# Five of the 32 float64 pieces narrowed among the retention's tiles in written order, the other 27 spread wider

## The chip, the cores and the metric

The kernel runs on one core of a Trainium2 chip. The metric is the device time of one execution in microseconds (us); lower is better. The core has TensorE (PE, matrix products), VectorE (DVE), ScalarE (ACT), GpSimd (POOL) and SyncE (SP), which issues most transfers. Each engine works through its own queue in order; they wait for each other by semaphores.

## What is computed

Three stages follow one another. A retention (attention with a decay instead of a softmax) over 4 x 8 heads of 576 positions gives 2304 tokens of 512 features. A mixture of 8 experts gives each token to one expert, at most 288 to each, by the order of all logits. A dense layer with a gate ends it; its weights w_in and w_out come as float64 words, the others as float32.

```python
rel = pos[:, None] - pos[None, :]
Dmat = np.where(rel >= 0, gamma[:, None, None] ** rel[None, :, :], 0.0)
x = np.matmul(scale * np.matmul(q, k.transpose(0, 1, 3, 2)) * Dmat, v)   # per head, then 2304 x 512
...
for idx in np.argsort(-(x @ w_gate).flatten()):                          # greedy, 288 tokens per expert
    ...
for e in range(E):
    out[mask] = np.maximum(x[mask] @ w1[e], 0.0) @ w2[e]
...
h = out @ w_in                                                           # w_in, w_out: float64
g = h * np.tanh(np.log1p(np.exp(h)))
return (g @ w_out).astype(np.float32)
```

## The kernel before

**Retention (0 to 82 us).** 18 tiles of 128 tokens, two in each pass of the loop `for o in range(2, NT, 2)`. For a tile t: `load` brings qk and kv (512 KB each, on SyncE), `scores` multiplies queries and keys on TensorE and puts the mask on with VectorE (am, L200), `scale` makes qs and ks on GpSimd (L185, L188), `carried` and `outputs` form the output pT from the running state S and from am, ScalarE copies it (xT, L238), `state` adds to S (L214, VectorE), `turn` turns xT into rows of tokens with the router's logits (pX, L248; L, L250 on VectorE; xs, L252 on ScalarE), `store` sends xs to DRAM. TensorE, VectorE, GpSimd and SyncE take this stage's instructions in the order in which the code is written (`manual_schedule`).

**Routing (82 to 119 us).** The greedy order is found by a serial chain of short steps, mostly on VectorE (L394 to L541), with tiny products on TensorE (small). It starts in the last pass of the retention for the first 16 tiles (L380 to L406, G) and goes on after the last logits. After the first expert is known, the steps for the next ones (known, sat, scan, ohb, pI, chosen) run beside the experts.

**Experts (119 to 362 us).** For each expert GpSimd gathers its 288 tokens (xg, L651), TensorE turns them (mmx, L672), ScalarE and VectorE split them into a high and a low part (xh L662, xl L664), and TensorE multiplies in three passes: 96 products mma for the first layer (then hh on ScalarE, hl on VectorE), 96 products mmb for the second, whose result y is copied by ScalarE (L849) out of one of five banks. Weights come in units of 512 KB (st, issued by SyncE at L588); ScalarE makes whi (L602) of each, VectorE or GpSimd wlo (L605), which frees the place of st. The last units (`final_units`) are the narrowed w_in and w_out.

**Narrowing.** w_in and w_out are 32 pieces of 128 x 512 float64 numbers (512 KB). One piece takes a load std (L762, issued on ScalarE's queue for the piece three further on), words on ScalarE (L779, a copy of the high words with a scale), a shift on VectorE (L781), a join with the low words on VectorE (dw, L784), the sign on ScalarE (dt, L788), a product with the sign on GpSimd (L798), and a store of 256 KB into a scratch tensor in DRAM (L767). All 32 are done beside the experts.

The order from the routing on is made by a planner when the program is built (`run_tasks`): of the tasks that can start, it takes the one that starts first by its own table of durations, unless one of higher priority comes soon. Narrowing has the low priority 4 and rises to `UP` when the number of narrowed pieces falls behind TensorE's planned time (`PACE` per piece, `START`). Transfers issued by SyncE and ScalarE take turns on eight completion semaphores, so an issue can wait for the landing of the transfer eight places before it, whichever of the two queues that was on.

```python
    def narrow_priority(self):
        return UP if len(self.features) >= URGENT or len(self.narrowed) * PACE + START < self.time.get(PE, 0) else 4
```

Of the kernel before, what the change touches and what calls it, by code (L numbers as in the profile page):

```python
# [7 lines left out]
F32 = mybir.dt.float32  # L8
# [3 lines left out]
U32 = mybir.dt.uint32  # L12
# [42 lines left out]
EID = -2  # L55
PACE = 8000
START = 50000
# [76 lines left out]
class Kernel:  # L134
# [3 lines left out]
    def attention(self):  # L138
# [7 lines left out]
        with ExitStack() as st:  # L146
# [3 lines left out]
            ps = st.enter_context(tc.tile_pool(name="ps", bufs=1, space=PSUM))  # L150
            st.enter_context(tc.manual_schedule(engines={mybir.EngineType.PE, mybir.EngineType.DVE, mybir.EngineType.Pool, mybir.EngineType.SP}))
            dec = one.tile([P, DCN], F32, name="dec")
# [103 lines left out]
            def store(t):  # L256

                if t in XS:
                    nc.sync.dma_start(a["x"][t * P:(t + 1) * P, :], XS.pop(t))
# [36 lines left out]
            for o in range(2, NT, 2):  # L296
                b = o + 1
                load(o + 4)
                load(o + 5, "qk")
                if o + 4 >= NT:  # L300
                    for t in range(o):
                        store(t)
                scores(b)
                carried(o)
                carried(b)
                scores(b + 1)
                if o == 6:
# [12 lines left out]
                if b < NT - 1:  # L320
                    state(b)
                outputs(b)
                if b + 1 < NT - 1:
                    state(b + 1)
                turn(o)
                if b < NT - 1:
                    turn(b)
            t = b
            self.psum = lambda name, shape: ps.tile(shape, F32, name=name, tag="pS", bufs=1)
# [3 lines left out]
            for i in range(NT):  # L333
                store(i)
            self.choices(late, choice)
            self.reached(choice, G, late)
# [342 lines left out]
    def narrow_priority(self):  # L679
        return UP if len(self.features) >= URGENT or len(self.narrowed) * PACE + START < self.time.get(PE, 0) else 4  # L680

# [55 lines left out]
    def step(self, t, done):  # L737
        try:
            t[0] = t[1].send(done)
        except StopIteration:  # L740
            self.tasks.remove(t)

    def narrow(self):

        nc, v, ic, a = self.nc, self.nc.vector, self.ic, self.a
        done = {k: {} for k in ("load", "read", "turn", "shift", "sign", "store")}

        def at(k, n):
            return [lambda: done[k].get(n)] if n >= 0 else []

        name = ("w_in", "w_out")
        words, sent = {}, {}

        def place(n):
            c, r = divmod(n // 2, a[name[n % 2]].shape[0] // P)
            return name[n % 2], slice(r * P, r * P + P), c

        def fetch(n, queue):
            if n < 32:
                w, r, c = place(n)  # L760
                words[n] = self.conv.tile([P, 512, 2], U32, name="std", bufs=3)
                queue.dma_start(words[n].rearrange("p c w -> p (c w)"), a[w].bitcast(U32)[r, c * 1024:c * 1024 + 1024])  # L762

        def send(n, queue):
            if n >= 0:
                w, r, c = place(n)
                queue.dma_start(a[w + "32"][r, c * 512:c * 512 + 512], sent.pop(n))  # L767

        def load():
            now = yield SP, 3 * DMA_ISSUE, [Event(0)], self.narrow_priority  # L770
            for n in range(3):
                fetch(n, nc.sync)
                self.spawn(piece(n, self.arrival(524288, now, LATE)))

        def piece(n, now):
# [15 lines left out]
            fetch(n + 3, nc.scalar)  # L791
            if n:
                self.narrowed[n - 1] = done["store"][n - 1] = self.arrival(262144, sign, LATE)
# [367 lines left out]
```

## Time and profile before

| what | value |
|---|---|
| median of 3 runs | 790.85 us (790.5 to 792.45) |
| profiled execution | 792.95 us, span of its instructions 791.2 us |
| TensorE busy | 749.2 us, 95% |
| VectorE busy | 672.9 us, 85% |
| ScalarE busy | 405.5 us, 51% |
| GpSimd busy | 488.1 us, 62% |
| moved by DMA | 111.94 MB, 141 GB/s over the span |

The span runs from the first to the last instruction of the profiled execution; its time is that of the whole execution. A row of a timeline gives the start in us from the span's start, the duration in us, engine, line and operation, and in square brackets the idle time of the engine ahead of the instruction and what ended it.

### The profile page before, as it was taken

What the parts mean: (1) busy time and instruction counts of PE and PEld (TensorE: products, weight loads), DVE (VectorE), ACT (ScalarE), POOL (GpSimd) and SP (SyncE); (2) the same over time, 40 slices, a digit from 0 to 9 for tenths busy, and PEclk for the clock granted to TensorE, in tenths of its full rate; (3) what the DMA queues carried; (4) which work ended last, traced back from release to release, by engine and by line L of the source; (5) the groups of instructions that cost most, each with busy time, mean ns of one, the idle gap of its engine ahead of it and who ended that gap; (6) DMA issues with size and microseconds to landing.
All of it is one profiled execution on the core that took longest, in us unless ns stands there. A gap on an engine that the chain in (4) does not pass through costs nothing.

```text
span 791.2 us, 15556 instructions
## 1 busy us (share of the span) xinstructions
PE 749.2 (95%) x5892; PEld 679.0 (86%) x5892; DVE 672.9 (85%) x1079; ACT 405.5 (51%) x783; POOL 488.1 (62%) x408
## 2 busy tenths in 40 slices
PE   7999379999999999799999999999999999999995
PEld 5999239899898999799998999899999989998983
DVE  4445788888898888777999999989999998998993
ACT  2333025646556475757764465546555554655451
POOL 6651036979788797430577586557557655756554
PEclk9999699999999999999999999999999999999998
DMA  9887085888888888986500011010001001001001
GB/s 359 327 291 268 28 271 185 278 266 281 274 291 278 273 279 270 334 283 213 174 22 22 1 50 31 1 41 30 12 1 51 31 0 41 21 1 40 1 1 40
DMA packets 60539, 111.94 MB, mean 141 GB/s; under 512 B 4784, under 2 KB 32432, under 8 KB 60464
## 3 DMA queue, kind: packets, MB, share of 16 engines
q1 hardware_dynamic: 44240, 73.45, 27.4%
q10 hardware_dynamic: 13248, 28.06, 10.1%
q0 software_dynamic: 2976, 9.44, 3.7%
q8 instruction: 46, 0.75, 0.4%
q14 instruction: 29, 0.24, 0.1%
HBM read 88.38 MB, written 22.54 MB: 140 GB/s over the span
## 4 chain that ended last, share of the span: by engine, by line
PE 46%; DVE 12%; DMA 2%; ACT 2%; issue 1%; POOL 1%; ACTq 0%; POOLq 0%; SPq 0%; DVEq 0%
PE mmc L1038 20%; PE po L1099 19%; DVE q L1068 6%; PE mma L815 4%; DVE n L1063 3%; PE mmb L815 2%; DMA st<-w 1%; ACT whi L602 1%; DVE n L1073 1%; DVE wlo L605 1%; DMA q<-y_scratch 1%; POOL gl L1080 1%; POOL n L1070 0%; DVE G L472 0%; DVE words L781 0%
## 5 line engine op out<-in xcount | busy, mean ns | idle before, releaser
L1068 DVE RECIPROCAL q<-q 128x384 f32<-128x384 f32 x96 | 243.8, 2540 | 0.1
L1070 POOL TENSOR_TENSOR n<-n,q 128x384 f32<-128x384 f32 x96 | 101.1, 1054 | 161.6 <-DVE q L1068 142.7
L605 POOL TENSOR_TENSOR wlo<-st,whi 128x1024 fp32r<-128x1024 f32 x51 | 122.4, 2414 | 16.7 <-ACT whi L602 11.7
L1038 PE MATMUL mmc<-yh,whi 128*128 128x384 f32 x384 | 129.6, 337 | 1.0 <-DVE n L1073 1.0
L1038 PE MATMUL mmc<-yl,whi 128*128 128x384 f32 x384 | 129.9, 338 | 0.2 <-DVE yl L998 0.2
L1038 PE MATMUL mmc<-yh,wlo 128*128 128x384 f32 x384 | 129.4, 337 | 0.0
L1078 ACT CAST gh<-n 128x384 fp32r<-128x384 f32 x96 | 49.3, 513 | 148.3 <-DVE n L1073 141.0
L1080 POOL TENSOR_TENSOR gl<-n,gh 128x384 fp32r<-128x384 f32 x96 | 120.2, 1254 | 3.6 <-ACT gh L1078 3.5
L1063 DVE SCALAR_TENSOR_TENSOR n<-s 128x384 f32<-128x384 f32 x96 | 114.9, 1198 | 5.2 <-POOL gl L1080 3.9
L1099 PE MATMUL po<-whi,gl 128*128 128x512 f32 x288 | 114.9, 399 | 1.4 <-POOL gl L1080 1.0
L1099 PE MATMUL po<-whi,gh 128*128 128x512 f32 x288 | 114.5, 397 | 0.7 <-ACT gh L1078 0.7
L1099 PE MATMUL po<-wlo,gh 128*128 128x512 f32 x288 | 113.9, 396 | 0.0
L602 ACT CAST whi<-st 128x1024 fp32r<-128x1024 f32 x80 | 82.7, 1044 | 34.7 <-issue 23.7
L815 PE MATMUL mma<-xh,whi 128*128 128x288 f32 x256 | 77.9, 304 | 3.4 <-ACT xh L662 2.6
L815 PE MATMUL mma<-xl,whi 128*128 128x288 f32 x256 | 77.3, 302 | 1.9 <-DVE xl L664 1.9
L815 PE MATMUL mmb<-hl,whi 128*128 128x288 f32 x256 | 77.3, 302 | 0.0
L815 PE MATMUL mmb<-hh,whi 128*128 128x288 f32 x256 | 77.1, 301 | 0.0
L815 PE MATMUL mma<-xh,wlo 128*128 128x288 f32 x256 | 77.1, 301 | 0.0
L1038 PEld LDWEIGHTS mmc<-yh,whi 128*128 128x128 f32 x384 | 72.1, 188 | 5.3 <-DVE n L1073 1.4
L1038 PEld LDWEIGHTS mmc<-yl,whi 128*128 128x128 f32 x384 | 72.1, 188 | 4.5 <-DVE yl L998 0.4
L815 PE MATMUL mmb<-hh,wlo 128*128 128x288 f32 x256 | 75.9, 296 | 0.0
L1038 PEld LDWEIGHTS mmc<-yh,wlo 128*128 128x128 f32 x384 | 72.1, 188 | 0.0
(153 smaller groups left out, 1548.9 us busy)
## 6 DMA issues: line engine op xcount, KB each, us to landing
st<-w SPq DMA_DIRECT2D x64, 512.0 KB
qk<-qk SPq DMA_DIRECT2D x18, 512.0 KB
kv<-kv SPq DMA_DIRECT2D x18, 512.0 KB
std<-w_out ACTq DMA_DIRECT2D x15, 512.0 KB
std<-w_in ACTq DMA_DIRECT2D x14, 512.0 KB
x_scratch<-xs SPq DMA_DIRECT2D x18, 256.0 KB
y_scratch<-y ACTq DMA_DIRECT2D x32, 144.0 KB
yt<-y_scratch SPq DMA_DIRECT2D x22, 192.0 KB
```

What stands on the lines that cost most here:

```text
L602: self.nc.scalar.copy(dst[0], st)
L605: (self.nc.vector if lo.engine == DVE else self.nc.gpsimd).tensor_tensor(dst[1], st, dst[0].bitcast(F32), op=ALU.subtract)
L815: self.nc.tensor.matmul(bank[1][:, :CAP], al if h == 2 else ah, bl if h == 1 else bh, start=(first and j == h == 0), stop=(last and j == n ...
L1038: self.nc.tensor.matmul(bank[1][:, :TILE], (wl if h == 2 else wh)[:, c, cs], x[c][h == 1], start=(c == h == 0), stop=(c == HP - 1 and h == 2))
L1063: v.scalar_tensor_tensor(u, s, 2.0, s, op0=ALU.subtract, op1=ALU.mult)
L1068: v.reciprocal(q, q)
L1070: nc.gpsimd.tensor_tensor(u, u, q, op=ALU.mult)
L1073: v.tensor_tensor(u, u, p, op=ALU.mult)
L1078: nc.scalar.copy(gh, u)
L1080: nc.gpsimd.tensor_tensor(gl, u, gh.bitcast(F32), op=ALU.subtract)
L1099: nc.tensor.matmul(po[j], (gl if h == 2 else gh)[:, js], (wl if h == 1 else wh)[:, f % 2], start=(f == h == 0), stop=(f == DFF // P - 1 an ...
```

## The change

`EARLY` = 5 pieces (n = 0 to 4) are narrowed in the retention, one for each pass from o = 8 to o = 16 (`FROM` = 8). `early_pieces` returns five steps, which the loop calls at fixed places: `load_piece(o + 2)` and `send_piece(o - 2)` on SyncE behind the next tiles' loads, `shift(o)` on VectorE between the mask products of the pass's two tiles, `join(o)` on VectorE between its two copies of S, with the product by the sign on GpSimd behind it, and `widths(o + 2)` (words and sign) on ScalarE at the end of the pass. The last store stands behind the stores of x. ScalarE's order in the retention is now the written one too. The early pieces have tiles of their own (est 3, ewords 2, edt 1, edw 3). The planner does the other 27, with `PACE` at 9500 instead of 8000, counted from `EARLY` on.

```diff
-PACE = 8000
+PACE = 9500
+EARLY = 5
+FROM = 8
...
                 load(o + 4)
                 load(o + 5, "qk")
+                load_piece(o + 2)
+                send_piece(o - 2)
...
                 carried(o)
                 carried(b)
+                shift(o)
                 scores(b + 1)
...
                 if b < NT - 1:
                     state(b)
+                join(o)
                 outputs(b)
...
                 turn(o)
                 if b < NT - 1:
                     turn(b)
+                    widths(o + 2)
...
             for i in range(NT):
                 store(i)
+            send_piece(b - 1)
...
-        return UP if len(self.features) >= URGENT or len(self.narrowed) * PACE + START < self.time.get(PE, 0) else 4
+        return UP if len(self.features) >= URGENT or (len(self.narrowed) - EARLY) * PACE + START < self.time.get(PE, 0) else 4
...
+        def load(n):
+            st[n] = pool.tile([P, 512, 2], U32, name="est", bufs=3)
+            nc.sync.dma_start(st[n].rearrange("p c w -> p (c w)"), self.piece_of(n)[0])
+
+        def widths(n):
+            high = st[n][:, :, 1].bitcast(F32)
+            words[n] = pool.tile([P, 512], F32, name="ewords", bufs=2)
+            nc.scalar.activation(words[n], high, AF.Copy, scale=2.0 ** -112)
+            sign[n] = pool.tile([P, 512], F32, name="edt", bufs=1)
+            nc.scalar.sign(sign[n], high)
+
+        def shift(n):
+            w = words[n].bitcast(U32)
+            nc.vector.tensor_scalar(w, w, self.ic[:, IC["three"]], None, op0=ALU.logical_shift_left)
+
+        def join(n):
+            o = pool.tile([P, 512], U32, name="edw", bufs=3)
+            nc.vector.scalar_tensor_tensor(o, st[n][:, :, 0], self.ic[:, IC["low"]], words[n].bitcast(U32),
+                                           op0=ALU.logical_shift_right, op1=ALU.bitwise_or)
+            out[n] = o.bitcast(F32)
+            nc.gpsimd.tensor_tensor(out[n], out[n], sign[n], op=ALU.mult)
...
+        def step(of):
+            def run(o):
+                if 0 <= (o - FROM) // 2 < EARLY:
+                    of((o - FROM) // 2)
+            return run
...
-            for n in range(3):
+            for n in range(EARLY, EARLY + 3):
                 fetch(n, nc.sync)
```

In the orders that follow, those after carry the line numbers of the changed code. VectorE in the pass o = 14 of the retention, before (am the mask products, S the state, L the logits):

```order
L200 TENSOR_TENSOR am<-pA_88,mask_81 128x512
L200 TENSOR_TENSOR am<-pA_89,mask_81 128x512
L200 TENSOR_TENSOR am<-sc,mask_81 128x512
L200 TENSOR_TENSOR am<-pA_88,mask_81 128x512
L214 TENSOR_TENSOR S<-pS,dec 128x256 x2
L250 TENSOR_REDUCE L<-pX 128x8 x2
```

And after (ewords is what the shift works on, edw the join's result):

```order
L203 TENSOR_TENSOR am<-pA_91,mask_84 128x512
L203 TENSOR_TENSOR am<-pA_92,mask_84 128x512
L776 TENSOR_SCALAR ewords<-ewords,consts 128x512
L203 TENSOR_TENSOR am<-sc,mask_84 128x512
L203 TENSOR_TENSOR am<-pA_91,mask_84 128x512
L217 TENSOR_TENSOR S<-pS,dec 128x256
L780 SCALAR_TENSOR_TENSOR edw<-est,consts,ewords 128x512
L217 TENSOR_TENSOR S<-pS,dec 128x256
L253 TENSOR_REDUCE L<-pX 128x8 x2
```

The shift has come ahead of the third mask product, the join between the two copies of S.

VectorE in the last pass, before, from its last mask products over the routing's first steps (G is the last of them) to the last logits:

```order
L200 TENSOR_TENSOR am<-pA_89,mask_81 128x512
L200 TENSOR_TENSOR am<-sc,mask_81 128x512
L380 TENSOR_SCALAR sc<-consts 128x194
L394 TENSOR_REDUCE sc<-L 128x16
L396 TENSOR_TENSOR sc<-L,sc 128x128
L397 TENSOR_TENSOR sc<-sc,consts 128x128
L398 TENSOR_REDUCE top<-sc 128x16
L399 TENSOR_TENSOR oh<-sc,top 128x128
L406 TENSOR_TENSOR G_123<-sc,consts 128x16x63
L250 TENSOR_REDUCE L<-pX 128x8 x2
L394 TENSOR_REDUCE sc<-L 128x2
```

And after:

```order
L203 TENSOR_TENSOR am<-pA_92,mask_84 128x512
L203 TENSOR_TENSOR am<-sc,mask_84 128x512
L776 TENSOR_SCALAR ewords<-ewords,consts 128x512
L389 TENSOR_SCALAR sc<-consts 128x194
L403 TENSOR_REDUCE sc<-L 128x16
L405 TENSOR_TENSOR sc<-L,sc 128x128
L406 TENSOR_TENSOR sc<-sc,consts 128x128
L407 TENSOR_REDUCE top<-sc 128x16
L408 TENSOR_TENSOR oh<-sc,top 128x128
L415 TENSOR_TENSOR G_126<-sc,consts 128x16x63
L780 SCALAR_TENSOR_TENSOR edw<-est,consts,ewords 128x512
L253 TENSOR_REDUCE L<-pX 128x8 x2
```

The shift has come ahead of the routing's first step, the join between G and the last two rows of logits.

ScalarE where expert 5 ends and expert 6 begins, before (y the last copy of expert 5's result, xh the tokens of expert 6, dt, words and the DMA of w_in, w_out and std the narrowing, whi a weight unit, hh the first result of expert 6):

```order
L849 COPY y<-mmb_5221 128x288
L851 DMA y_scratch<-y 128x288
L662 CAST xh<-mmx_5328 128x288
L662 CAST xh<-mmx_5336 128x288
L662 CAST xh<-mmx_5341 128x288
L662 CAST xh<-mmx_5346 128x288
L788 ACTIVATE dt<-std 128x512
L767 DMA w_in<-dw 128x512
L762 DMA std<-w_in 128x1024
L602 CAST whi<-st 128x1024
L838 ACTIVATE hh<-mma_5356 128x288
```

And after:

```order
L671 CAST xh<-mmx_5335 128x288
L671 CAST xh<-mmx_5340 128x288
L671 CAST xh<-mmx_5345 128x288
L671 CAST xh<-mmx_5350 128x288
L836 ACTIVATE dt<-std 128x512
L815 DMA w_out<-dw 128x512
L811 DMA std<-w_out 128x1024
L827 ACTIVATE words<-std 128x512
L897 COPY y<-mmb_5258 128x288
L899 DMA y_scratch<-y 128x288
```

The last y copy has moved from ahead of xh to behind a piece's fetch (DMA std) and words.

TensorE at the same place, before (mmb the last product of expert 5, mmx the turning of tokens, mma expert 6's first layer):

```order
L815 MATMUL mmb_5221<-hh,wlo 128x288
L672 MATMUL mmx_5328<-consts,xg 128x96 x3
L672 MATMUL mmx_5336<-consts,xg 128x96 x3
L672 MATMUL mmx_5341<-consts,xg 128x96 x3
L672 MATMUL mmx_5346<-consts,xg 128x96 x3
L815 MATMUL mma_5356<-xh,whi 128x288
L815 MATMUL mma_5356<-xl,whi 128x288
```

And after:

```order
L863 MATMUL mmb_5258<-hh,wlo 128x288
L681 MATMUL mmx_5390<-consts,xg 128x96 x3
L681 MATMUL mmx_5394<-consts,xg 128x96 x3
L681 MATMUL mmx_5398<-consts,xg 128x96 x3
L681 MATMUL mmx_5404<-consts,xg 128x96 x3
L863 MATMUL mma_5409<-xh,whi 128x288
L863 MATMUL mma_5409<-xl,whi 128x288
```

The tokens turned here are now those of expert 7 (before, its four mmx stood behind 22 products mma of expert 6), and those of expert 6 stand 12 products earlier, among the mmb. Further ahead, the 18 products pI for expert 7 stood behind 39 products mmb of expert 5 and now stand behind 20. Behind the place of expert 7's mmx in the order before, the rows of TensorE are the same in both.

## Rows read from the trace of the kernel before

**Rows 1.** The page's slices: busy tenths of TensorE in 40 slices.

```profile
PE   7999379999999999799999999999999999999995
```

**Rows 2.** Stretches: length; busy PE, PEld, DVE, ACT, POOL; clock, DMA share, GB/s.

```profile
10.00:20.00 10.00, 9.99 (x176) 8.75 (x173) 5.39 (x11) 1.94 (x6) 6.89 (x6) 1.00 1.02 411
40.00:50.00 10.00, 10.00 (x154) 9.26 (x154) 4.12 (x10) 3.79 (x13) 6.12 (x7) 1.00 0.85 303
60.00:70.00 10.00, 10.00 (x172) 9.03 (x174) 4.55 (x10) 2.59 (x8) 3.51 (x3) 1.00 0.76 256
140.00:312.00 172.00, 165.99 (x1730) 157.08 (x1729) 150.29 (x478) 102.24 (x182) 144.68 (x84) 1.00 0.84 277
312.00:330.00 18.00, 13.24 (x91) 12.44 (x91) 11.73 (x20) 12.24 (x23) 7.46 (x5) 0.91 1.00 347
```

**Rows 3.** Waits of TensorE, 120 to 312 us: total us, times, longest.

```profile
PE small L490 <- DVE known L477: 3.3, 8, 0.6
PE small L495 <- DVE sat L411: 1.5, 5, 0.5
```

**Rows 4.** Groups by line, 119 to 362 us: busy us, mean ns, idle before.

```profile
L779 ACT ACTIVATE words<-std 128x512 f32<-128x512 f32 x32 | 20.5, 642 | 27.6 <-DMA st<-w 16.8 <-ACT dt L788 5.8 <-DVE sat L411 4.2
L788 ACT ACTIVATE dt<-std 128x512 f32<-128x512 f32 x32 | 21.8, 681 | 0.4 <-ACT y L849 0.4
L781 DVE TENSOR_SCALAR words<-words,consts 128x512 uint32<-128x512 uint32 x32 | 24.0, 751 | 3.4 <-ACT words L779 3.4
L784 DVE SCALAR_TENSOR_TENSOR dw<-std,consts,words 128x512 uint32<-128x512 uint32 x32 | 23.9, 746 | 1.1
L798 POOL TENSOR_TENSOR dw<-dw,dt 128x512 f32<-128x512 f32 x32 | 44.0, 1375 | 16.5 <-ACT dt L788 12.2 <-ACT y L849 2.7 <-DMA w_out<-dw 1.2
```

**Rows 5.** Timeline of VectorE in two passes of the retention.

```profile
64.24 0.42 DVE L214 TENSOR_TENSOR S<-pS,dec 128x256 f32<-128x256 f32 x1 [1.06 <-PE pS L211]
69.49 0.69 DVE L200 TENSOR_TENSOR am<-sc,mask 128x512 f32<-128x512 f32 x1 [0.84 <-PE pA L197]
72.34 0.42 DVE L214 TENSOR_TENSOR S<-pS,dec 128x256 f32<-128x256 f32 x1 [0.91 <-PE pS L211]
```

**Rows 6.** Timeline of ScalarE in the pass about 70 us.

```profile
70.59 0.65 ACT L238 COPY xT<-pT 128x256 f32<-128x256 f32 x2 [3.45 <-PE pT L234]
```

**Rows 7.** Timeline of GpSimd, its last scaling in the retention.

```profile
62.60 2.51 POOL L185 TENSOR_TENSOR qs<-qk,dec 128x512 f32<-128x512 f32 x2
```

**Rows 8.** Timeline of VectorE at the end of the retention.

```profile
78.77 1.20 DVE L406 TENSOR_TENSOR G<-sc,consts 128x1008 bf16<-128x1008 f32 x1
79.89 0.16 DVE L250 TENSOR_REDUCE L<-pX 128x8 f32<-128x16 f32 x1
80.45 0.17 DVE L250 TENSOR_REDUCE L<-pX 128x8 f32<-128x16 f32 x1 [0.41 <-PE pX L248]
```

**Rows 9.** Timeline of ScalarE at the start of expert 6.

```profile
323.62 1.05 ACT L602 CAST whi<-st 128x1024 fp32r<-128x1024 f32 x1 [3.79 <-DMA st<-w]
```

**Rows 10.** The chain of waits at that place: start us, us, what.

```profile
306.65 0.49 PE pI L639 x18
308.00 3.50 DVE wlo L605 x3
311.52 11.63 DMA st<-w
327.02 9.87 PE mma L815 x72
336.89 12.79 PE mmb L815 x96
```

**Rows 11.** Timeline of TensorE at the start of expert 6.

```profile
318.42 0.40 PE L815 MATMUL mma<-xh,whi 128*128 128x288 f32 x1 [2.63 <-ACT xh L662]
319.49 0.54 PE L815 MATMUL mma<-xl,whi 128*128 128x288 f32 x1 [0.68 <-DVE xl L664]
322.95 0.33 PE L815 MATMUL mma<-xh,whi 128*128 128x288 f32 x1
```

More of the change, by code (lines that the diff above doesn't have):

```diff
@@ L150, in attention @@
             ps = st.enter_context(tc.tile_pool(name="ps", bufs=1, space=PSUM))
-            st.enter_context(tc.manual_schedule(engines={mybir.EngineType.PE, mybir.EngineType.DVE, mybir.EngineType.Pool, mybir.EngineType.SP}))
+            st.enter_context(tc.manual_schedule(engines={mybir.EngineType.PE, mybir.EngineType.DVE, mybir.EngineType.Pool, mybir.EngineType.SP, mybir.EngineType.Activation}))
+            load_piece, widths, shift, join, send_piece = self.early_pieces(st.enter_context(tc.tile_pool(name="early", bufs=1)))
             dec = one.tile([P, DCN], F32, name="dec")
@@ L741, in step, with piece_of, early_pieces, send @@
             self.tasks.remove(t)
+    def piece_of(self, n):
+        name = ("w_in", "w_out")[n % 2]
+        c, r = divmod(n // 2, self.a[name].shape[0] // P)
+        rows = slice(r * P, r * P + P)
+        return self.a[name].bitcast(U32)[rows, c * 1024:c * 1024 + 1024], self.a[name + "32"][rows, c * 512:c * 512 + 512]
+    def early_pieces(self, pool):
+        nc, st, words, sign, out = self.nc, {}, {}, {}, {}
+        def load(n):
[16 more added lines that the diff above has]
+            nc.gpsimd.tensor_tensor(out[n], out[n], sign[n], op=ALU.mult)
+        def send(n):
+            nc.sync.dma_start(self.piece_of(n)[1], out[n])
+        def step(of):
[3 more added lines that the diff above has]
+            return run
+        return [step(x) for x in (load, widths, shift, join, send)]
     def narrow(self):
@@ L746, in narrow @@
         done = {k: {} for k in ("load", "read", "turn", "shift", "sign", "store")}
+        for n in range(EARLY):
+            self.narrowed[n] = Event(0)
         def at(k, n):
-            return [lambda: done[k].get(n)] if n >= 0 else []
-        name = ("w_in", "w_out")
+            return [lambda: done[k].get(n)] if n >= EARLY else []
         words, sent = {}, {}
-        def place(n):
-            c, r = divmod(n // 2, a[name[n % 2]].shape[0] // P)
-            return name[n % 2], slice(r * P, r * P + P), c
         def fetch(n, queue):
             if n < 32:
-                w, r, c = place(n)
                 words[n] = self.conv.tile([P, 512, 2], U32, name="std", bufs=3)
-                queue.dma_start(words[n].rearrange("p c w -> p (c w)"), a[w].bitcast(U32)[r, c * 1024:c * 1024 + 1024])
+                queue.dma_start(words[n].rearrange("p c w -> p (c w)"), self.piece_of(n)[0])
         def send(n, queue):
-            if n >= 0:
-                w, r, c = place(n)
-                queue.dma_start(a[w + "32"][r, c * 512:c * 512 + 512], sent.pop(n))
+            if n >= EARLY:
+                queue.dma_start(self.piece_of(n)[1], sent.pop(n))
         def load():
             now = yield SP, 3 * DMA_ISSUE, [Event(0)], self.narrow_priority
-            for n in range(3):
+            for n in range(EARLY, EARLY + 3):
                 fetch(n, nc.sync)
@@ L791, in piece @@
             fetch(n + 3, nc.scalar)
-            if n:
+            if n > EARLY:
                 self.narrowed[n - 1] = done["store"][n - 1] = self.arrival(262144, sign, LATE)
```

## The prediction

> **What bounds the kernel now.** I read the slices first. Over the 40 slices, of 19.8 us each, TensorE's digit is 9 nearly throughout; inside the span it dips to 3 and 7 in slices 5 and 6 (the routing) and to 7 in slice 17 [rows 1]. So the time is TensorE's own work plus the holes in it, and since the change leaves TensorE's instructions as they are, it can only fill or open holes. The table of stretches says where they are [rows 2]: in the retention (40 to 50 and 60 to 70 us) TensorE is full while VectorE is busy for 4.1 and 4.6 of 10 us, ScalarE for 3.8 and 2.6 and GpSimd for 6.1 and 3.5; among the experts (140 to 312) TensorE is idle for 6.0 of 172 us beside a VectorE that is busy for 150.3; between 312 and 330, where expert 5 ends and expert 6 begins, it is idle for 4.8 of 18 us and its granted clock is 0.91. The waits of TensorE give the causes: among the experts the routing's steps on VectorE (known 3.3 us, sat 1.5) [rows 3], at the start of expert 6 first of all ScalarE's xh, 2.6 us [rows 11].
>
> **Narrowing one piece** costs 0.64 + 0.68 us on ScalarE, 0.75 + 0.75 us on VectorE, 1.38 us on GpSimd [rows 4], and 512 KB in and 256 KB out by DMA. Five pieces leave the experts and enter the retention. So 7.5 us of VectorE, 6.6 of ScalarE and 6.9 of GpSimd change their place, and 3.9 MB of DMA.
>
> **Retention, the pairs: 0.** A pair takes 8.1 us (second S at 64.24 and at 72.34) [rows 5]. Take the one about 70 us. Ahead of the third mask product, at 69.49, VectorE idles for 0.84 us, and ahead of the second S, at 72.34, for 0.91 [rows 5]. The shift (0.75) and the join (0.75) stand exactly in these two gaps, with 0.1 us to spare each. A slip of a few tenths there would delay an am that is used only by the pair's second tile. ScalarE waits for 3.45 us before xT [rows 6]: words and sign (1.3 us), which the new order puts right there, fit. GpSimd scales the queries of the last two tiles at 62.60 and ends at 65.11 [rows 7], although TensorE uses them only in the last pair, of which the mask products start behind the S of 72.34: it runs a pair ahead, and a product of 1.4 us in between is covered. The queue of SyncE gets one load and one store per pair ahead of the later kv load. Cost 0, as long as the DMA keeps up, which is the matter of rival (d).
>
> **End of retention: +1.0 us.** The last piece's shift and join stand in the last iteration, where VectorE has no gap: the last am, L380 and seven instructions of the routing stand back to back, G at 78.77, then L250 at 79.89 [rows 8]. Behind it the routing's chain begins, and TensorE waits for that. The shift comes ahead of L380 and the join between G and L250. Instructions that stand back to back start up to 0.08 us before the one ahead ends (78.77 + 1.20 against 79.89), so the two add 1.34 to 1.50 us; the second L250 had waited 0.41 us for TensorE, which is now over. That makes 0.9 to 1.1, and 1.5 at most if TensorE slips along. Taken: +1.0. Nothing behind takes it back: the routing is serial down to the first expert.
>
> **Among the experts: -0.3 us.** Some four pieces instead of five fall to an expert. VectorE's 150.3 us in 172 fall by four or five times 1.5, or 6 to 7.5 us, 4 to 5% of its load; if the 6.0 us of TensorE's waits on it [rows 3] fall in proportion, that is 0.3 us. These waits end a chain of short routing steps, and a piece hurts only where it stands within such a chain, so they need not fall at all, and could fall by half where the planner no longer puts a piece there: bounds -3.0 and 0. Against it, the ends of experts 4 and 5 in the new order have the last y copy right ahead of the next expert's first product, behind a fetch; some tenths each, up to +1.0.
>
> **Expert 5 to 6: -0.5 us.** Here is the largest hole. A cast whi on ScalarE had waited 3.79 us behind a piece's fetch (L762) [rows 9]. The chain of waits names the reason [rows 10]: the pI products of expert 7 release VectorE, whose three wlo (308.00 + 3.50) free the slot of a weight load; this is issued at 311.52 and lands 11.63 us later, at 323.15; then the fetch goes, and whi at 323.62. So hh is late behind them, and TensorE waits. Now the new order. A fetch that waits for the same weight load stands ahead of the last y copy of expert 5, and expert 6's first product needs that copy's bank; in the order before, that copy stood ahead of the fetch and 22 products ran before the hole. In return the 18 pI products for expert 7 come after 20 instead of 39 products of expert 5's second layer. A product takes 12.79 / 96 = 0.133 us [rows 10], so they come 19 x 0.133 = 2.5 us earlier, and with them the chain on VectorE that ends in the three wlo and the weight load. The load would land at 320.6, the fetch (0.34), words (0.64) and y (0.40) follow, and expert 6 begins at 322.0 with all 96 products: 322.0 + 12.8 = 334.8. Before, the last 72 began at 327.02 and ended at 336.89 [rows 10]. What remains is the clock. After 2.63 us of idleness, the 14 matmuls from 319.49 up to the one at 322.95 took 3.46 us, 0.247 each, at the lower of the two levels, 1.2 GHz [rows 11]: 14 x (0.247 - 0.133) = 1.6 us. Now TensorE would idle for longer in one piece (from the end of the second layer at 318.42 - 2.63 = 315.79, plus a microsecond of mmx, to 322.0), and so starts slow again: 334.8 + 1.6 = 336.4, against 336.89, or -0.5. Bounds: the fetch finds the load landed and nothing stops, the idle 4.8 us and the slow clock's 1.6 are gone, -6.4; the load lands no earlier than before, because VectorE is busy without a break up to it, 2.5 worse than that, +2.0; the slow clock lasts twice as long, another +1.6, in all +3.6.
>
> **The sum** is +1.0 - 0.3 - 0.5 = +0.2 us. The profiled run took 792.95 us (span 791.2 and 1.75 around it), 2.1 above the median of 790.85; by this sum it would take 793.15, and the median 791.05. Forecast: **791.0 us, no change**. About 0.3% (2.4 us) is what a measurement of this kernel can tell from no change.
>
> **The rivals.** (a) **No hole at expert 6.** For it: the weight load is issued 2.5 us sooner, there is less DMA beside it (768 KB for each piece that is gone), and the hole was an accident of one queue order. Against it: in the new order the fetch still stands in front of what TensorE needs, and the load took 11.63 us, as DMA was at 1.00 of its share between 312 and 330 [rows 2]. Time: 790.85 + 1.0 - 0.3 - 6.4 = 785.2. (b) **Freed engines.** The steady waits fall by half, -3.0: 790.85 + 1.0 - 3.0 - 0.5 = 788.4. For it speaks that these waits end on VectorE [rows 3]; against it that VectorE had 22 idle us in that stretch already [rows 2]. (c) **Slower: the y copy behind the fetch.** The weight load doesn't land earlier, since VectorE has hardly a gap in front of the three wlo; ScalarE holds the y copy, expert 6 begins late with all 96 products and a cold clock: 790.85 + 1.0 - 0.3 + 2.0 to 3.6 = 793.6 to 795.2. It takes the lead from the point at which the load lands less than 2 us earlier than before. (d) **Slower: the retention's loads run late.** A piece adds 0.79 MB to a pair of 8.1 us, 97 GB/s. On the 303 GB/s of 40 to 50 us and the 256 of 60 to 70 [rows 2] that gives 400 and 353. By the share of 0.85 that went with 303, a full share is 356 GB/s; the 411 of the stretch 10 to 20, at a share of 1.02, says that more goes through. At 356 GB/s the shortfall of 40 to 60 us is at most 44 GB/s x 20 us = 0.9 MB or 2.5 us, and a lead of a pair, 8 us [rows 5, 7], covers it. Only if late pieces hold ScalarE's queue, with xT behind them, does it show: 791.05 + 2.5 = 793.6.
>
> The Trainium skill, "DMA: Bandwidth & Descriptors", section Specifications, gives about 358 GB/s as the limit of HBM for one core. The trace moved 411 GB/s for 10 us [rows 2], so it doesn't bind here by the measurement; by the rule (d) would have its shortfall for sure.
>
> (e) **It doesn't do what it says**: the planner, with its pace changed, puts the 27 pieces where 32 stood. Five pieces less are then a pure change of place, and the sum is the first term alone, 791.9, within the forecast's bound.
>
> **How the numbers follow.** Forecast, with (e): 0.45. (a) 0.10 and (b) 0.20 are the faster cases: 0.30. (c) 0.15 and (d) 0.10 are the slower ones: 0.25. The range leaves out (a) and the far end of (c): 787.0 to 794.5.
>
> **What the profile after would show.** Shift and join in VectorE's two gaps of a pair and a pair period of 8.1 us: right; a longer period or xT waiting behind words on a DMA: (d). The first routing step about 1.0 us later: right. TensorE's idle time among the experts between 5 and 7 us: right; 3: (b). At the start of expert 6 a wait on ScalarE of several us, then matmuls 0.24 us apart: right or (c), told apart by when the weight load lands; no wait: (a). What would make the prediction wrong is above all this one place: it holds 6 us up or 3 down, and rests on the order of one queue and on the landing of one load.

## The result, and the profile after

The changed kernel takes 799.15 us (median of 6 runs, 797.92 to 801.78) against 790.85: ratio 1.0108, interval 1.0087 to 1.0129. It is slower by 8.3 us. The prediction, no change with a range up to 794.5, was wrong. The profiled execution took 801.78 us, of which the instructions span 800.0 (before 792.95 and 791.2).

Where the time came from is read from TensorE's own marks: its first product of expert 0, the end of expert 5's second layer, the end of expert 6's first layer, and the end (before at 119.38, 314.80, 336.89 and 791.2 us, after at 121.58, 324.74, 346.03 and 800.0).

| stretch | before, us | after, us | difference |
|---|---|---|---|
| start to expert 0 (retention, routing) | 119.38 | 121.58 | +2.2 |
| expert 0 to the end of expert 5 | 195.42 | 203.16 | +7.7 |
| end of expert 5 to the end of expert 6's first layer | 22.09 | 21.29 | -0.8 |
| from there to the end | 454.27 | 453.95 | -0.3 |

The line between the two middle rows moves some work. The 12 products that turn expert 6's tokens, 1.0 us, stand behind the end of expert 5 in the order before and ahead of it in the new one. With them counted among the experts in both, the two rows are +6.8 and +0.2. So most of it is among the experts. The page shows it as two 8s in TensorE's slices 13 and 14 (240 to 280 us), where before had 9s [rows 1]; PEclk is the granted clock in tenths:

```profile
PE   8999389999998899799999999999999999999995
PEclk9999689999999999899999999999999999999998
```

The table of stretches after, to be held against [rows 2]: of the 172 us from 140 to 312, before had TensorE busy for 166; here it is busy for 57.39 + 54.13 + 46.38 of the 170 us up to 310, so idle for 12.1. VectorE is busy for 139 of those 170 us: it is not full.

```profile
core 0: us, PE busy (x) PEld busy (x) DVE busy (x) ACT busy (x) POOL busy (x), PEclk, DMA share, GB/s
140.00:200.00 60.00, 57.39 (x609) 54.02 (x606) 51.84 (x169) 35.99 (x63) 51.04 (x30) 1.00 0.79 262
200.00:260.00 60.00, 54.13 (x585) 50.81 (x583) 47.15 (x151) 30.36 (x54) 46.83 (x28) 1.00 0.80 258
260.00:310.00 50.00, 46.38 (x467) 44.69 (x468) 40.28 (x146) 25.25 (x44) 38.00 (x22) 0.97 0.74 240
```

TensorE's waits from 119 to 312 us, against 3.3 us for known, 1.5 for sat [rows 3] and 1.2 for xl before:

```profile
PE small L499 <- DVE known L486: 5.9, 10, 1.2
PE small L504 <- DVE sat L420: 5.1, 5, 2.1
PE mma L863 <- DVE xl L673: 0.5, 2, 0.3
PE small L528 <- DVE scan L525: 0.4, 1, 0.4
```

That is 11.9 us instead of 6.0, so 5.9 more. The longest wait for sat is 2.1 us; there are two such, at 244 and 279. Behind the second the clock is granted at half for 3.5 us (1.2 instead of 2.4 GHz), which costs half of that, 1.7 us:

```profile
280.60:284.10 3.50, 3.50 (x32) 3.35 (x31) 2.87 (x6) 0.62 (x1) 3.50 (x2) 0.51 0.31 107
```

5.9 + 1.7 = 7.6 us, which covers the 6.8; where the other 0.8 came back isn't traced. Now one of the two waits itself, on the three engines that take part. TensorE: 18 small products, four products of the layer, then the wait:

```profile
240.76 0.60 PE L499 MATMUL small<-oh,G 128*128 128x8 bf16 x18
241.22 0.38 PE L863 MATMUL mmb<-hh,whi 128*128 128x288 f32 x1
241.44 0.30 PE L863 MATMUL mmb<-hl,whi 128*128 128x288 f32 x1
241.57 0.29 PE L863 MATMUL mmb<-hh,wlo 128*128 128x288 f32 x1
241.71 0.29 PE L863 MATMUL mmb<-hh,whi 128*128 128x288 f32 x1
244.03 0.17 PE L504 MATMUL small<-sat,digit 128*128 128x8 bf16 x1 [2.03 <-DVE sat L420]
```

VectorE, which makes sat out of those small products, idles for 2.64 us ahead of it, and the trace names no engine of this core as the releaser:

```profile
239.19 1.33 DVE L481 TENSOR_TENSOR G<-sc,consts 128x1134 bf16<-128x1134 f32 x1
240.44 0.73 DVE L832 SCALAR_TENSOR_TENSOR dw<-std,consts,words 128x512 uint32<-128x512 uint32 x1
243.81 0.17 DVE L420 TENSOR_SCALAR sat<-small 128x8 bf16<-128x8 f32 x1 [2.64 <-remote]
```

GpSimd at that time issues the three gathers of the next expert's tokens:

```profile
239.54 0.94 POOL L660 DMA_INDIRECT xg<-x_scratch,chosen  x1 [5.64 <-DVE chosen L652]
240.78 0.92 POOL L660 DMA_INDIRECT xg<-x_scratch,chosen  x1 [0.30 <-issue]
242.01 0.92 POOL L660 DMA_INDIRECT xg<-x_scratch,chosen  x1 [0.30 <-issue]
242.95 1.29 POOL L846 TENSOR_TENSOR dw<-dw,dt 128x512 f32<-128x512 f32 x1
```

The 18 products end at 241.36. VectorE takes sat at 243.81, 0.9 us after the last gather's issue is over. The trace's record of the semaphore that sat waits for, and that the last of the 18 products raises, is at 243.79. So TensorE's update is 2.4 us late, and TensorE then waits for an engine that waited for TensorE. In the kernel before, the same lateness can be found once one looks for it, but smaller. There VectorE's sc, at 273.89, waits for the product of L495, which had run from 273.15 to 273.32, while gathers ran from 271.79 on. TensorE had other products to do at that moment, and paid further down the chain, where known came late and it waited 0.57 us:

```profile
272.94 0.16 DVE L411 TENSOR_SCALAR sat<-small 128x8 bf16<-128x8 f32 x1
273.89 0.17 DVE L456 TENSOR_REDUCE sc<-small 128x1 uint32<-128x8 f32 x1 [0.79 <-PE small L495]
276.38 0.61 PE L490 MATMUL small<-oh,G 128*128 128x8 bf16 x18 [0.57 <-DVE known L477]
```

### The profile page after: what moved, and what is told of

It is laid out like the page before. It is cut to its first block, busy times and chain, and to the rows that moved or that the text cites. A ratio compares the mean times of both kernels' runs of the same rounds, so it can differ in the third digit from the quotient of the medians.

```text
span 800.0 us, 15518 instructions
## 1 busy us (share of the span) xinstructions
PE 752.1 (94%) x5888; PEld 682.2 (85%) x5892; DVE 670.1 (84%) x1079; ACT 406.1 (51%) x783; POOL 486.2 (61%) x408
## 4 chain that ended last, share of the span: by engine, by line
PE 33%; DVE 27%; DMA 4%; POOL 4%; ACT 3%; issue 3%; another core or an unknown queue 1%; ACTq 0%; POOLq 0%; SPq 0%; DVEq 0%
DVE q L1116 14%; PE mmc L1086 11%; PE po L1147 11%; DVE n L1111 6%; PE mma L863 6%; PE mmb L863 4%; DVE n L1121 2%; DMA st<-w 2%; DMA yt<-y_scratch 1%; DVE G L481 1%; POOL gl L1128 1%; DMA std<-w_out 1%; POOL n L1118 1%; DVE wlo L614 1%; POOL out L1161 1%
## 5 line engine op out<-in xcount | busy, mean ns | idle before, releaser
L1116 DVE RECIPROCAL q<-q 128x384 f32<-128x384 f32 x96 | 243.8, 2540 | 0.0
```

The source lines that it names most:

```text
L1116: v.reciprocal(q, q)
```

## The experiments

The theory after this comparison: **the order, not the work.** PACE at 9500 puts the routing's round trip (18 products, sat, a product, sc, known) beside the gathers, where TensorE's updates come late. Rivals: **the early pieces** cost the time in the retention, or **the chip** was a different one.

Chips matter here. The kernel before takes 790.8 us on the chip of the first comparison and on that of b2_before below (which may be the same one), and 786.2 to 787.0 on four others. The difference that was found between the traces is this: on the former, TensorE's updates are 0.4 to 2.5 us late beside every expert's gathers (counted in the traces by the end of each product against the update); on the other four none is late by over 0.3 us. "A chip with late updates" means the former. Runs are compared only with before on the same chip.

**The pace and the pieces apart.** Three kernels on a chip without late updates (before 786.44).

e3_pace8000: the change, but

```diff
-PACE = 9500
+PACE = 8000
```

> The change with PACE back at 8000: five pieces early, the other 27 planned at the old pace, TensorE's order that of before but for 4 rows. Theory O: TensorE's waits on sat and known among the experts fall back to about 5 us, what is left is the retention's +2 and the hole at expert 6: 790 to 794 us. Rival R: 797 to 800 us.

e4_before9500: before, with the pace alone.

```diff
-PACE = 8000
+PACE = 9500
```

> The kernel before with PACE 9500 alone: no early pieces, all 32 in the planner, TensorE's order that of the changed kernel row by row. Theory O: the two waits of 2 us on sat at experts 4 and 5 are there, 795 to 799 us. Rival R: 790 to 792 us.

e1_extra: before, its planner doing all 32 pieces, and the five early pieces beside them as additional work with their results stored elsewhere.

> The kernel before, with five pieces narrowed in the retention as extra work (into a scratch of their own that nobody reads); the planner still does all 32 at PACE 8000. TensorE's order is that of before. Theory O (the loss is the new order among the experts that PACE brings): only the retention's part shows, +1.5 to +2.5 us, 792.5 to 793.5. Rival R (the work in the retention is what costs: its DMA, its queues, and what it starts late): 797 to 800 us.

| kernel | us | ratio to before | interval |
|---|---|---|---|
| e3_pace8000: pieces, old pace | 787.0 | 1.0008 | 0.9994 to 1.0023 |
| e4_before9500: new pace, no early piece | 790.09 | 1.0052 | 1.0028 to 1.0076 |
| e1_extra: five more pieces of work | 787.54 | 1.0017 | 1.0004 to 1.003 |

The pace alone costs 3.65 us; the early pieces with the old pace cost nothing that can be measured, and five pieces of extra work cost 1.1 us. TensorE's order follows from PACE: with 8000 it is that of before but for four lines, with 9500 that of the change, whether pieces are early or not. The waits from 119 to 312 us agree. e3_pace8000:

```profile
PE small L504 <- DVE sat L420: 1.3, 5, 0.3
PE mma L863 <- DVE xl L673: 1.2, 5, 0.3
PE small L499 <- DVE known L486: 0.6, 2, 0.4
```

e4_before9500:

```profile
PE small L490 <- DVE known L477: 2.4, 5, 0.6
PE small L495 <- DVE sat L411: 1.0, 4, 0.4
PE mma L815 <- DVE xl L664: 0.5, 2, 0.3
```

So the new order makes TensorE wait for known even where updates are punctual, 1.8 us more than the old one. The two waits of 2 us for sat that were expected of e4_before9500 aren't there. A second part of its 3.65 us is the clock, which is granted at half from 206.6 to 210.0 us; that costs 1.7 us, and in the 5 us ahead of it TensorE had no wait over 0.4 us. With the old order e3_pace8000 was run again on three chips, with a trace each time: 786.82 (1.0004, 0.9988 to 1.002), 786.36 (0.9993, 0.9981 to 1.0005) and 786.8 (1.0002, 0.9986 to 1.0018). What was expected:

> The change with PACE 8000 again, since e3_pace8000 ran on a chip on which no update of TensorE came late and the kernel took 786.4 before. On a chip with late updates: within 1.5 us of the kernel before if the new order is the cause there too (no wait of 2 us on sat), +8 if it is the early work.

> The change with PACE 8000 once more: on a chip with late updates within 1.5 us of the kernel before if the new order of the routing steps is what the late updates hit, +8 if the early work is; on the other kind of chip +0.5 as twice before.

> The change with PACE 8000 once more, for a chip on which TensorE's updates beside the gathers come late (the kernel before takes 790.8 there). By the theory that the loss is the new order's, it stays within 0.3% of before there too: 789 to 793, with no wait of 2 us for sat. By the rival that the early pieces cost more where updates are late, it is 794 or more. On a chip without late updates (786.3) it repeats 786.4 to 787.0 and tells nothing new.

None of the three fell on such a chip.

**The chip with late updates.** Here before took 790.81, and four kernels ran. Before and the change, once more:

> The kernel before once more, for its trace beside the others of this run, since the runs so far were on two chips. In the first pair of traces TensorE's semaphore updates came 0.5 to 2.5 us late while a gather was issued by GpSimd, in the later four they did not. Both theories: ratio 1.000 within 0.2%; if no update comes late here, TensorE's second layer of an expert takes 16.9 us instead of 17.7.

> The changed kernel once more beside them. Theory O (the order that PACE 9500 brings costs 4 to 5 us and the retention 1 to 2) gives +5 to +6.5 us where no update of TensorE comes late, and +8 where they do, since the round trip from TensorE to VectorE and back then stands 2 us at experts 4 and 5. Rival R (the retention) gives +8 in both.

e2_left: the change with its pace, but the five early pieces are not narrowed at all; only their five stores remain, of a constant tile.

```diff
-        return [step(x) for x in (load, widths, shift, join, send)]
+        none = lambda n: None
+        return [step(x) for x in (none, none, none, none, send)]
```

> The changed kernel with the five early pieces not narrowed at all (their part of the weights is left out; only the five stores stand, of a constant tile). TensorE's order is that of the changed kernel. Theory O: 1 to 2 us under the changed kernel, 3.5 to 5 us over the kernel before. Rival R: as before, within 1 us.

e6_nogather: the change, the gathers replaced by plain loads on SyncE's queue, so the experts get other tokens.

```diff
-            nc.gpsimd.indirect_dma_start(out=xg[:, j], out_offset=None, in_=a["x"],
-                                         in_offset=bass.IndirectOffsetOnAxis(ap=idx[:, j:j + 1], axis=0))
+            nc.sync.dma_start(xg[:, j], a["x"][(3 * i + j) * GB % (N - GB):(3 * i + j) * GB % (N - GB) + GB, :])
```

> The changed kernel with the gathers by GpSimd replaced by plain loads from SyncE (the tokens are then not those that the routing chose; this part of the computation is left out). Theory O with late updates as their cause: where updates come late in the changed kernel beside this one, they come in time here, TensorE's waits on sat fall to 0.3 us each, and 3 to 5 us go; where they don't come late, 0 to 1 us. Rival (the late updates have nothing to do with the gather): they stay.

| kernel | us | ratio to before | interval |
|---|---|---|---|
| b2_before | 791.96 | 1.0007 | 0.9993 to 1.0021 |
| a2_after | 799.92 | 1.0102 | 1.0075 to 1.0129 |
| e2_left: the change without its five pieces | 800.22 | 1.011 | 1.0087 to 1.0133 |
| e6_nogather: the change without gathers | 785.79 | 0.9916 | 0.9885 to 0.9947 |

Two things follow. Leaving the early pieces out gives nothing back, where 1 to 2 us had been expected: the loss isn't theirs. (In the traces e2_left begins expert 0 at 119.43 us and a2_after at 121.31; e2_left loses these 1.9 us again behind expert 5.) And taking the gathers away gives 14 us back, where 3 to 5 had been expected. Not all of it is lateness, as the next runs show. In a2_after the wait of the first comparison is there again, at the same place:

```profile
243.52 0.17 DVE L420 TENSOR_SCALAR sat<-small 128x8 bf16<-128x8 f32 x1 [2.65 <-remote]
```

and in e6_nogather, with the same order on the same chip, sat waits for its 18 products only:

```profile
240.00 0.17 DVE L420 TENSOR_SCALAR sat<-small 128x8 bf16<-128x8 f32 x1 [0.23 <-PE small L499]
```

Among the experts no update of e6_nogather is late. That ties the lateness to the gathers. e6_nogather takes GpSimd's issue, its descriptors and the indirect transfer away all at once, and the tokens no longer wait for the routing, so which of these it is stays open.

**The change and the gathers on chips without late updates.** a3_after is the change again (before 786.31); e6b_nogather is e6_nogather again, e7_bnogather and e7b_bnogather are before with the same plain loads (before 786.18, 786.98 for the last).

> The changed kernel once more. On a chip on which no update of TensorE comes late (the kernel before then takes about 786): if late updates are the larger part of its loss, +1 to +4.5 us over the kernel before (PACE alone gave +4.1 there, the retention's part about +1, five pieces fewer some back); on a chip with late updates +8 to +9 again.

> The kernel before with the gathers replaced by plain loads from SyncE, as in e6_nogather (the tokens are not those that the routing chose; left out). Late updates of TensorE go here too, but the order of before lost less to them. If the late updates were the whole loss of the change, this and the changed kernel without gathers take the same time within 1 us; if the order costs by itself as well, this one is 3 to 5 us faster than the changed kernel without gathers.

> The changed kernel without gathers once more, beside e7_bnogather on one chip: 3 to 5 us slower than that if the order costs by itself, the same within 1 us if only the late updates cost.

> The kernel before with the gathers replaced by plain loads (wrong rows come to the experts). By the theory that gathers make TensorE's updates late, and that this is the whole of the distance between 790.8 and 786.3, it takes 786 to 787 where before takes 790.8. By the rival that such a chip is slower throughout, it stays above 789. On a chip without late updates: 786.1 again.

| kernel | us | ratio to before | interval |
|---|---|---|---|
| a3_after | 791.77 | 1.0067 | 1.0045 to 1.0089 |
| e7_bnogather: before without gathers | 786.12 | 1.0002 | 0.9988 to 1.0016 |
| e6b_nogather: the change without gathers | 784.86 | 0.9983 | 0.9969 to 0.9996 |
| e7b_bnogather, another chip | 785.31 | 0.9981 | 0.9966 to 0.9996 |

Even without late updates the change is slower, by 5.5 us; 1 to 4.5 had been expected. So the late updates are not its whole loss. Between the two kinds of chips the change differs by 8.1 us (799.92 against 791.77) and the kernel before by 4.5 (790.8 against 786.3). Without gathers the change differs by 0.9 (785.79 against 784.86, the latter on another chip without late updates). So of the 14 us that e6_nogather gained, about 7 go with the lateness, and a3_after and e6b_nogather are the other 6.9 apart where no update is late. In a3_after sat waits 0.23 us, though it stands just as near to the gathers (235.98 to 239.38):

```profile
237.84 0.17 DVE L420 TENSOR_SCALAR sat<-small 128x8 bf16<-128x8 f32 x1 [0.23 <-PE small L499]
```

The 5.5 us are other things there. TensorE waits 2.7 us for known (0.4 in e3c_pace8000, the old order on the same chip), and the hole between experts 5 and 6 is long:

```profile
317.72 2.18 PE L681 MATMUL mmx<-consts,xg 96*128 96x96 f32 x12 [2.55 <-DVE xl L673]
321.55 0.61 PE L863 MATMUL mma<-xh,whi 128*128 128x288 f32 x1 [1.65 <-ACT y L897]
```

The two traces of that chip differ as follows: a3_after begins expert 0 1.1 us before e3c_pace8000 (120.44 against 121.53), begins expert 5 0.9 behind it (285.61, 284.76), so it lost 1.9 among the experts; it ends expert 6's first layer 4.8 behind it (335.95, 331.16), so 3.9 at the hole; and at the end it is 2.4 behind, because e3c_pace8000 lost 2.4 later (below). Of the 3.9 us, 2.6 are the clock: in a3_after it is granted at half from 317.7 to 324.6, of which TensorE is busy for 5.2; e3c_pace8000 has the full clock there.

But e3c_pace8000 is not before, and its hole is a short one. e1_extra, which has the order of before (on another chip without late updates), takes 49.8 us from expert 5's first product to the end of expert 6's first layer, a3_after 50.3 and e3c_pace8000 46.4. From expert 0's first product to expert 5's it takes 162.7, a3_after 165.2 and e4_before9500 166.3. So against the order of before the traces show the loss among the experts, 2.4 to 3.5 us, and hardly any at the hole. Not all of the 5.5 us is found: a3_after's traced execution took 790.84 us, 0.9 less than its median.

Without gathers the new order isn't slower at all (784.86 against 786.12). It still waits 2.3 us for known there (e7_bnogather 0.4) and is 1.7 us longer up to expert 5; it gains 2.0 at the hole, which has 1.0 us of waits. Before, on the other hand, neither loses nor gains much without gathers where updates are punctual (1.0002 on one chip, 0.9981 on another). Before without gathers was not seen on a chip with late updates, so how much of the distance of 790.8 to 786.2 the late updates explain isn't shown by a run. The trace of b2_before has 4.6 us of waits for known where e7_bnogather has 0.4, which would be most of it.

**A better place for the pieces.** The hole at expert 6 has pieces' fetches in it. So the last pieces may be the ones to take out, not the first.

e5_last: pieces 27 to 31 early, old pace.

```diff
-                    of((o - FROM) // 2)
+                    of(LAST + (o - FROM) // 2)      # LAST = 32 - EARLY
...
-            for n in range(EARLY, EARLY + 3):
+            for n in range(3):
```

> The last five pieces instead of the first five are narrowed in the retention, PACE 8000: the planner does pieces 0 to 26 in the order of before, and no fetch stands at the place where expert 6 begins. Theory O: retention +2 us, the hole at expert 6 (4.8 us and the slow clock's 1.6) mostly gone: 786 to 789 us. Rival R: 795 us or more, since the retention does the same as in the changed kernel.

It took 787.46 (before 786.44; 1.0011, 0.9996 to 1.0025): no gain, although it ended expert 6's first layer at 329.65, against 334.00 in e1_extra, which has before's order and was on the same chip. Its traced execution was 2.6 us below that of e1_extra, but its median is that of e1_extra (787.54) within 0.1, so a part of what the trace shows gained isn't in the median, and where it goes isn't shown. In the trace 1.7 us went behind expert 6, in the dense layer's first tiles. There VectorE (q, L1116 of the change, 244 us in 96 instructions) sets the pace, and TensorE waits for the first yh instead (e5_last, between 345 and 380 us; e3c_pace8000 has 2.0 us there):

```profile
PE mmc L1087 <- ACT yh L1044: 1.6, 1, 1.6
```

e8_last4: as e5_last with EARLY = 4, so that no piece stands in the last pass, in which VectorE had no gap [rows 8]; TensorE's order is that of before.

> A version meant to be faster: the last four pieces (28 to 31) are narrowed in the retention's passes o = 8 to 14, none in the last pass, PACE 8000. TensorE's order is that of before row by row, and the fetch at the start of expert 6 (that of piece 28) is gone. Theory: nothing is added ahead of the routing, so the retention costs 0 to 1 us; at expert 6 three of the five us of waiting go and the slow clock with them: 3 to 5 us under the kernel before. Rival: the hole moves on and comes back at the first dense tiles, where the token loads or VectorE are then late, and the time is that of before within 1 us.

> The version with the last four pieces early, once more: 1 to 4 us under the kernel before on either kind of chip, since its order is that of before and the fetch at expert 6 is gone.

> The last four pieces early, none in the last pass, TensorE's order that of before. Where updates are late: its gain lies at the start of expert 6, which has no gather beside it, so it should hold: 788 to 789.5 against 790.8. By the rival that the late updates swallow it, 790.5 to 791.5. On a chip without late updates: 784.4 to 784.8 again.

| run | us | before | ratio | interval |
|---|---|---|---|---|
| e8_last4 | 784.42 | 786.18 | 0.9971 | 0.9957 to 0.9984 |
| e8b_last4, another chip | 784.81 | 786.31 | 0.9976 | 0.9965 to 0.9988 |
| e8c_last4, a third | 783.88 | 786.98 | 0.9961 | 0.9944 to 0.9977 |

It beats before by 1.5 to 3.1 us on three chips (3 to 5 had been expected of the first), and so also the change. At expert 6 its waits, 312 to 345 us, are

```profile
PE mma L864 <- ACT xh L672: 1.6, 1, 1.6
PE mma L864 <- DVE xl L674: 0.7, 1, 0.7
```

and the dense layer begins without one. All three chips were without late updates; where they come late it was not run.

## Why the prediction was wrong

**The wrong step is "Among the experts: -0.3 us"**, where +6.8 was measured (expert 6's 12 token products counted here, as in the order before). It took the waits behind the routing's steps as something that scales with VectorE's load. VectorE's load did fall (its busy share from 150.3 of 172 us [rows 2] to 139.3 of 170), and the waits doubled. What set them was where the round trip TensorE, VectorE, TensorE stands in TensorE's order, and beside what: without early pieces the loss is the same (e2_left), and with the old order it is gone (e3_pace8000, on chips without late updates). The prediction had only the fetch and the y copy in view as effects of the new order, with bounds of -3.0 to +1.0. The order shows the rest: one number of the planner (PACE) moves every step of the routing, and I had costed it by the pieces it was meant to space. A sign of what was coming stood in the trace of before: beside the gather at 273 us, a product that ends at 273.32 and is seen only at 273.89, and behind it 0.57 us of the 3.3 that TensorE waited for known [rows 3]. I had read the waits of TensorE, but not the waits on TensorE.

**End of retention, +1.0 us**: right in kind, and more than twice too large. VectorE in the last pass after, against [rows 8]:

```profile
77.75 0.48 DVE L776 TENSOR_SCALAR ewords<-ewords,consts 128x512 uint32<-128x512 uint32 x1
...
80.12 1.20 DVE L415 TENSOR_TENSOR G<-sc,consts 128x1008 bf16<-128x1008 f32 x1
81.24 0.74 DVE L780 SCALAR_TENSOR_TENSOR edw<-est,consts,ewords 128x512 uint32<-128x512 uint32 x1
81.89 0.24 DVE L253 TENSOR_REDUCE L<-pX 128x8 f32<-128x16 f32 x2
```

Shift and join stand where the order put them, back to back; the shift takes 0.48 us here, not the 0.75 that I took from the experts. By these rows the two cost 0.39 + 0.65 (start to start) less the 0.41 that the last logits had waited anyway, or 0.6 us. The traces fix the size. From the start of the last S to the end of the last logits it is 8.72 us in all eleven that have a piece in the last pass, and 8.29 in all nine that have none: +0.4 us. The first product of expert 0 came 2.2 us later. Of this, 1.1 us were there at the last S (next paragraph), 0.4 are the last piece, and 0.7 came in the routing, where the clock was granted at half from 113.4 to 116.8 us and before it was full from 110 on. In the medians the pieces cost less than that: e1_extra +1.1, a2_after against e2_left -0.3.

**Retention, the pairs, 0**: too low. The second S of a pair stands at 73.42 us, before at 72.34 [rows 5], and 0.7 of these 1.1 us come in one pass, of 9.6 us instead of 8.9. There TensorE stops for 1.0 us in the middle of a group of 16 products, and no engine explains it; a2_after has the stop with 0.7, up to the same 64.72:

```profile
63.31 0.39 PE L214 MATMUL pS<-kv,ks 128*64 128x64 f32 x6
64.72 0.56 PE L214 MATMUL pS<-kv,ks 128*64 128x64 f32 x10 [1.01 <-issue]
65.32 0.42 DVE L217 TENSOR_TENSOR S<-pS,dec 128x256 f32<-128x256 f32 x1 [0.92 <-PE pS L214]
```

Without pieces this pass takes 8.4 or 8.9 us in six traces; with pieces 8.0 to 9.9. Why TensorE stops is open. The join of that pass took 1.56 us beside a ks on GpSimd, not 0.75; S waited for TensorE behind it.

**Expert 5 to 6, -0.5 us**: measured +0.2 (-0.8 in the table, less the 1.0 us of moved products), by the predicted mechanism. ScalarE after:

```profile
320.98 0.34 ACTq L811 DMA_DIRECT2D std<-w_in  x1
321.37 0.40 ACT L897 COPY y<-mmb 128x288 f32<-128x288 f32 x1 [0.41 <-PE mmb L863]
323.65 0.33 ACTq L899 DMA_DIRECT2D y_scratch<-y  x1
324.02 1.05 ACT L611 CAST whi<-st 128x1024 fp32r<-128x1024 f32 x1 [2.25 <-DMA st<-w]
...
329.61 0.34 ACTq L811 DMA_DIRECT2D std<-w_out  x1
330.00 0.62 ACT L827 ACTIVATE words<-std 128x512 f32<-128x512 f32 x1 [3.17 <-DMA st<-w]
330.56 0.39 ACT L897 COPY y<-mmb 128x288 f32<-128x288 f32 x1
```

and TensorE:

```profile
331.00 0.61 PE L863 MATMUL mma<-xh,whi 128*128 128x288 f32 x1 [2.69 <-ACT y L897]
```

The fetch waits for the landing of a weight load, words and the last y follow, and expert 6 begins 0.05 us behind y. From the end of the second layer to the first product: 331.00 - 324.74 = 6.3 us, predicted 322.0 - 315.79 = 6.2. The clock was at half for longer:

```profile
328.40:335.20 6.80, 4.20 (x17) 4.20 (x18) 3.53 (x8) 4.67 (x10) 1.29 (x1) 0.50 0.92 336
```

The 17 products in it cost 17 x 0.11 = 1.9 us, predicted 1.6. The fetch that waits for the weight load goes 4.9 us behind the end of the second layer (329.61 against 324.74), predicted 320.6 - 315.79 = 4.8. Rival (c), put at 2.0 to 3.6 us against before, didn't happen in the first comparison. On a chip without late updates the new order loses 3.9 us here to e3c_pace8000, but against the order of before (e1_extra) only 0.5.

**The rivals.** (a) and (b) fell: the hole stayed, and the waits rose. (b) in particular: more free time on VectorE did nothing for TensorE. (d) fell. All pairs but one kept their period, that one was held up by TensorE's stop and not by a load, and the page after has 340 and 370 GB/s in slices 3 and 4 (40 to 80 us). The Trainium skill, "DMA: Bandwidth & Descriptors", section Specifications, has about 358 GB/s as the limit; 370 over 20 us speaks against that here, as the 411 had. (e) fell as a cause: the planner does 27 pieces, and leaving the five out altogether (e2_left) changes nothing. Among the chances, slower had 0.25, but no case in it had this mechanism or this size: the case that was missing is that the moved order itself makes new waits.

**What stays open**: why some chips show late updates and others not; which part of a gather makes them late; whether e8_last4 and the change with the old pace hold on a chip with late updates.

## What to carry to other kernels

When a number that a planner reads is changed along with the work, run the number alone first: here the loss was there without the early work (e2_left, e4_before9500), and with the old number that work cost nothing measurable on four chips. Before trusting that an engine's short round trips (TensorE to VectorE and back) can be moved, look at what runs beside their new place, and read the waits of the other engines on the one that bounds. If work is to be taken out of a crowded stage, take the pieces that stand in its worst hole: four of them at the hole were worth 0.2 to 0.4%, five at the front nothing. Five at the hole (e5_last), one of them in the last pass, gave nothing either, so the place that they go to counts as well.

## What was not expected of the hardware

- TensorE's semaphore updates came up to 2.5 us late beside GpSimd's gathers on the chip of the first comparison and on that of b2_before, and on four others not at all, with the same program. The records of the products show them done (241.36), the engine behind started at 243.81.
- Where updates come late the second layer of experts 0 to 4 takes 17.7 us or more even with the old order, on the others mostly 16.9.
- The same shift of 128 x 512 words on VectorE took 0.48 us in three of the retention's five passes after (0.75 in the other two, beside a ks on GpSimd) and 0.75 each time among the experts, here with GpSimd idle. The join took 0.74 us, and 1.18 and 1.56 in two passes beside a ks on GpSimd:

```profile
62.84 1.56 DVE L780 SCALAR_TENSOR_TENSOR edw<-est,consts,ewords 128x512 uint32<-128x512 uint32 x1
246.87 0.75 DVE L829 TENSOR_SCALAR words<-words,consts 128x512 uint32<-128x512 uint32 x1
```
